# Compact states, paired outputs in rows of token parity with the bonus on TensorE, and a new order, in a chunked linear-attention kernel followed by a two-layer MLP

## The chip, the cores and the metric

The kernel runs on one core of a Trainium2 chip. The metric is the device time of one execution in microseconds (us). Engines are named as in the profile: PE (TensorE, matrix products; PEld are its weight loads), DVE (VectorE), ACT (ScalarE), POOL (GpSimd), SP (SyncE, which issues most DMAs). [...]

## The reference

B = 4 batches, H = 8 heads, S = 768 tokens, D = 48 columns a head; then an MLP of 384 -> 2048 -> 384 over 3072 tokens.

```python
state = zeros(B, H, D, D)
for t in range(S):
    cur = einsum('bhd,bhe->bhde', u[None] * k[t], v[t])
    y[t] = einsum('bhd,bhde->bhe', r[t], state + cur)
    state = w * state + einsum('bhd,bhe->bhde', k[t], v[t])
x = y, tokens as rows, heads side by side        # 3072 x 384
h = x @ w_in
g = where(h >= 1, h, where(h <= -1, 0, (h + 1)**2 / 4))
out = g @ w_out
```

## The kernel before

Tokens are cut into chunks of 128. A **group** is 256 tokens, and there are twelve. Groups 0 to 3 are **paired**: group g holds the first two chunks of batch g, with two neighbouring tokens (2q and 2q+1) in the same row; an index e or f of 2 is the parity of the token, and `un` (rows 0 to 63 or 64 to 127) tells the first chunk from the second. Groups 4 to 11 are unpaired: one chunk (c = 2 to 5) of each of two batches, index j.

The kernel's work is written as small steps, `step_X(e, s, g, ...)`. Their order is a list written out in the string `ORDER` (lines 32 to 67): a token such as `RU2@D` or `T0.0#3` is a step, its group (and half or quarter), after @ the engine (D VectorE, A ScalarE, P GpSimd) and after # one of four PSUM slots of two banks. Every engine runs its own instructions strictly in the order of this list, and each waits for what it reads and for the buffer that it writes. The steps of a group:

- `ldK`, `ldV`, `ldR`: loads, issued by SP in list order. `Vc`: V to bf16 (`Vb`).
- `Rs`, `Ks`: R and K times powers of the decay w, to bf16 (`RK`). `KU` = K times u, `RU` = R times KU, `us` sums RU over a head, `ud` = V times that sum: the bonus (`V2`). Group 0 is done in halves (.0 and .1).
- `T`, `TT`: RK transposed on TensorE, and copied out of PSUM (`RKT`). From group 4 on, `RK` does it with a DMA transpose.
- `A`, `AT`: products of K and R within a chunk, then masked on VectorE to bf16.
- `Sp`: K-transposed times V, the chunk's addition to the state, four pairs of heads. A pair is computed as one 96 x 96 block, so half of it, where the heads differ, is not wanted; `wCm` (the decay over a chunk) is zero there, and the product with it clears it. `Ta` (paired: first chunk's state), `Tm` (Sp plus state), `dc` (Tm times wCm) keep the state; `sa`, `sb` copy it to bf16.
- `Y`: the output of the group in PSUM: state part plus AT times Vb. `y` adds the bonus on VectorE, to bf16. `X`, `xT`: y transposed by TensorE (groups 0 to 3) or by DMA.
- `up` g.q: a quarter of the first layer, 12 matmuls of 256 columns; `re`, `sq` on ScalarE and `ga` on VectorE make the activation; `dn` g.j.q: four matmuls of 384 columns of the second layer; `o` copies out of PSUM, `st` stores.
- `wi`, `wo`: halves of w_in and w_out, loaded and converted by DMAs of GpSimd's queue. `kw`n: n matmuls of zeros, which write nothing that is used. `wr`, `ur`, `wB`, `uB`, `uc`, `ln`, `wu`, `wd`, `lp`, `lc`, `wc`: the tables of the decay and of u, from rows loaded on ScalarE's queue and spread by TensorE; `wB`, then `ln`, give log w, `wu` and `wd` the powers, `lc` and `wc` the chunk's decay `wCm`.

In a paired group, Y stands in PSUM with rows (chunk, q) and columns by parity f, so that a row of `out` for tokens 2q and 2q+1 lies in one partition.

Of the kernel before, what the change touches and what calls it, by code (L numbers as in the profile page):

```python
# [26 lines left out]

ORDER = """  # L30
wr@A ldK0.0 ldV0 ldR0.0 ur@A tb kw16#0 wB#0 uB#1 ln wu0 uc@D KU0.0@P wd1 wd0 wu1 lp ldK0.1 KU0.1@D Rs0.0@D RU0.0@P
Ks0.0@D kw20#2 lc#2 wc us0.0 ldR0.1 RU0.1@D ldR1 us0.1 Rs1@D Vc0@A ldK1 kw6#0 T0.0#3 Ks0.1@P Rs0.1@P kw13#0 T0.1#1
TT0.0@A TT0.1@A A0.0#0 Ks1@D Sp0#2 Ta0 ldV1 vu AT0.0 Vc1@A A0.1#3 Tm0 AT0.1 ud0.0@P ud0.1@D T1.0#1 TT1.0@A A1.0#0
sa0@A Y0.0#2 y0.0 Y0.1#1 y0.1 T1.1#3 TT1.1@D wi0 Sp1#2 Ta1 Tm1 AT1.0 wi1 wo0 KU1@P X0#1 dc0@P A1.1#3 AT1.1 sb0@A xT0@A
sa1@P up0.0#1 up0.1#2 Y1#0 RU1@P us1 ud1@D y1 up0.2#3 up0.3#0 re0.0 sq0.0 re0.1 sq0.1 ga0.0 ga0.1 X1#1 xT1@D up1.0#2
up1.1#1 re0.2 sq0.2 ga0.2 dc1@P sb1@P ldK2 KU2@P re0.3 sq0.3 dn0.0.0#3 dn0.1.0 dn0.1.1 ldR2 re1.0 sq1.0 Rs2@P Ks2@D
ga0.3 ga1.0 RU2@D re1.1 sq1.1 ga1.1 T2.0#0 TT2.0@A ldV2 Vc2@P up1.2#2 re1.2 Sp2#0 wo1 up1.3#1 ldR3 Rs3@P ldR4 Ta2 Tm2
dn0.0.1 ldR5 dn1.0.0#0 dn1.0.1 sq1.2 ga1.2 re1.3 sq1.3 us2 sa2@P ga1.3 T2.1#2 ldK3 dn1.1.0 dn1.1.1 A2.0#1 AT2.0
TT2.1@A A2.1#2 AT2.1 ldK4 dn0.0.2 dn0.0.3 dn1.1.2 dn1.0.2 Y2#1 Ks3@D ud2@P Rs4@P dc2@D y2 Rs5@P vd T3.0#2 TT3.0@D
dn1.1.3 dn1.0.3 o0.0@A o1.0@A KU3@P RU3@D X2#1 xT2@A A3.0#2 AT3.0 ldV3 Vc3@A o1.1@A dn0.1.2 dn0.1.3 Ks4@P us3 T3.1#1  # L40
TT3.1@A Sp3#2 o0.1@D Ta3 Tm3 up2.0#0 KU4@P A3.1#3 AT3.1 ldV4 Vc4@P Sp4#1 ud3@P RU4@P Tm4 up2.1#2 re2.0 sa3@A sq2.0
ga2.0 Y3#3 y3 re2.1 sq2.1 up2.2#1 up2.3#0 re2.2 X3#3 sq2.2 ga2.1 xT3@D us4 ldK5 dn2.0.0#2 dn2.0.1 up3.0#3 dn2.1.0
Ks5@P ga2.2 RK4 st0 ldV5 RK5 A4.0#1 re2.3 sq2.3 ldR6 dn2.1.1 ga2.3 A4.1#0 dc4@P sb2@P dc3@P dn2.1.2 dn2.0.2 re3.0
sq3.0 dn2.0.3 AT4.0 AT4.1 dn2.1.3 KU5@P RU5@P Y4#1 us5 up3.1#0 Vc5@A ga3.0 A5.0#3 st1 ud4@P y4 o2.0@A o2.1@A sb3@P
A5.1#2 re3.1 sq3.1 AT5.0 AT5.1 ldK6 up3.2#1 xT4 up3.3#3 ga3.1 dn3.0.0#2 dn3.1.0 sb4@P Rs6@P Y5#0 re3.2 sq3.2 ga3.2
dn3.0.1 dn3.0.2 ud5@D y5 up4.0#1 re3.3 sq3.3 ga3.3 ldK7 ldR7 dn3.1.1 Sp5#0 KU6@P Ks6@P KU7@P RU6@P up4.1#3 re4.0 sq4.0
re4.1 sq4.1 dn3.1.2 dn3.0.3 dn3.1.3 Tm5 ga4.0 us6 ga4.1 o3.0@A up4.2#0 o3.1@A RK6 A6.0#1 AT6.0 A6.1#2 re4.2 sq4.2
up4.3#3 AT6.1 xT5 up5.0#1 up5.1#2 RU7@P dc5@P ldV6 re4.3 sq4.3 ga4.2 ga4.3 us7 Rs7@P Vc6@P re5.0 sq5.0 ud6@P Ks7@D
dn4.0.0#0 dn4.1.0 dn4.1.1 dn4.1.2 dn4.0.1 ldR8 dn4.1.3 up5.2#3 dn4.0.2 dn4.0.3 st3 re5.1 sq5.1 Rs8@D ga5.0 ga5.1 Y6#1
y6 ldV7 st2 ldK8 re5.2 sq5.2 ga5.2 Ks8@D RK7 Vc7@P o4.0@A o4.1@A up5.3#2 re5.3 sq5.3 Sp6#0 dn5.0.0#1 dn5.0.1 dn5.1.0  # L50
dn5.1.1 A7.0#3 dn5.0.2 Tm6 sb5@A ud7@P KU8@P RU8@P dc6@P A7.1#0 ga5.3 xT6 up6.0#2 AT7.0 AT7.1 Sp7#3 dn5.0.3 ldV8 sb6@A
Y7#0 Tm7 re6.0 sq6.0 y7 dn5.1.2 dn5.1.3 Vc8@P o5.0@A Sp8#3 o5.1@A ga6.0 RK8 up6.1#0 re6.1 sq6.1 ldK9 Tm8 A8.0#1 AT8.0
A8.1#2 AT8.1 xT7 up6.2#3 re6.2 up6.3#1 dn6.0.0#2 dn6.1.0 sq6.2 ga6.1 us8 re6.3 sq6.3 ga6.2 ga6.3 ldR9 Rs9@D dn6.1.1
up7.0#0 re7.0 sq7.0 Y8#3 dn6.0.1 up7.1#1 KU9@P ud8@P st4 ldK10 re7.1 sq7.1 ga7.0 y8 ga7.1 RU9@P ldR10 Rs10@D dn6.0.2
dn6.0.3 up7.2#0 re7.2 dn6.1.2 o6.0@D Ks9@P RK9 up7.3#3 sq7.2 re7.3 sq7.3 ga7.2 dc8@P dc7@P sb7@P dn7.0.0#1 dn7.0.1
dn7.1.0 KU10@P dn6.1.3 o6.1@A A9.0#0 dn7.0.2 A9.1#2 dn7.1.1 ga7.3 dn7.0.3 xT8 up8.0#3 dn7.1.2 dn7.1.3 Ks10@P AT9.0
AT9.1 us9 ldV9 Vc9@P st5 o7.0@D o7.1@D ud9@P sb8@P Y9#0 y9 re8.0 sq8.0 ga8.0 up8.1#2 Sp9#1 Tm9 up8.2#0 up8.3#3 re8.1
dn8.0.0#1 dn8.1.0 ldR11 Rs11@P dc9@D st6 sq8.1 ga8.1 ldK11 RU10@D re8.2 sq8.2 xT9 ga8.2 us10 ldV10 re8.3 RK10 sq8.3
up9.0#2 dn8.0.1 up9.1#0 dn8.1.1 dn8.1.2 ga8.3 dn8.0.2 st7 Ks11@P KU11@P RU11@P RK11 A10.0#3 dn8.0.3 us11 re9.0 sq9.0
ga9.0 A10.1#2 AT10.0 AT10.1 dn8.1.3 re9.1 sq9.1 o8.0@A up9.2#3 re9.2 o8.1@D ga9.1 Vc10@P ud10@P Y10#2 y10 up9.3#1  # L60
sq9.2 re9.3 sq9.3 dn9.0.0#0 dn9.1.0 dn9.0.1 A11.0#2 dn9.1.1 ga9.2 sb9@A ldV11 Vc11@A A11.1#3 dn9.1.2 AT11.0 AT11.1
xT10 up10.0#2 re10.0 sq10.0 dn9.0.2 ga9.3 Y11#3 ud11@P y11 xT11 ga10.0 up10.1#1 dn9.0.3 up10.2#3 re10.1 dn9.1.3 o9.0@D
o9.1@D sq10.1 st8 st9 re10.2 ga10.1 sq10.2 ga10.2 up10.3#2 re10.3 sq10.3 ga10.3 up11.0#0 re11.0 sq11.0 dn10.0.0#1
dn10.1.0 dn10.1.1 dn10.0.1 dn10.0.2 up11.1#3 up11.2#2 re11.1 sq11.1 ga11.0 ga11.1 dn10.0.3 dn10.1.2 up11.3#0 re11.2
sq11.2 re11.3 sq11.3 ga11.2 dn10.1.3 dn11.0.0#3 dn11.1.0 dn11.0.1 o10.0@D o10.1@A st10 dn11.0.2 dn11.1.1 dn11.1.2
ga11.3 dn11.0.3 dn11.1.3 o11.0@A st11.0 o11.1@A st11.1
# [4 lines left out]
def kernel(  # L71
# [174 lines left out]
    def step_wu(e, s, i):  # L246
        if i == 0:
            nc.scalar.activation(flat(W2[0][:, 0]), lw, AF.Exp, scale=up2_col)
        else:
            nc.vector.tensor_mul(flat(W2[0][:, 1]), flat(W2[0][:, 0]), got("wB"))  # L250

    def step_wd(e, s, i):
        if i == 1:
            nc.scalar.activation(flat(W2[1][:, 1]), lw, AF.Exp, scale=dn2_col)
# [12 lines left out]
    def step_lc(e, s):  # L267
        col = bank(s, "lcol", (), [P, NP], F32)
        for p in range(NP):
            nc.tensor.matmul(col[:, p : p + 1], lwp[:, p].rearrange("q i d -> q (i d)"), ones[:, :1], start=True, stop=True)  # L270
# [8 lines left out]

    def step_wi(e, s, i):  # L280
        n = slice(i * DF // 2, (i + 1) * DF // 2)
        nc.gpsimd.dma_start(out=w_in_sb[:, :, n], in_=w_in_src[:, :, n])

    def step_wo(e, s, i):
        n = slice(i * nF // 2, (i + 1) * nF // 2)
        nc.gpsimd.dma_start(out=w_out_sb[:, n, :], in_=w_out_src[:, n, :])
# [83 lines left out]
    def step_A(e, s, g, h):  # L370
        t = got("RKT", g)
        if g in PAIRED:
            A = bank(s, "A", (g, h), [P, 2, NP // 2, 2, P], F32)
            for p in range(NP // 2):
                for e2 in range(2):
                    for i in range(2):
                        ps = slice(i * HP, i * HP + D)
                        for un in range(2):
                            q = slice(un * HP, (un + 1) * HP)
                            nc.tensor.matmul(  # L380
                                A[q, i, p, e2].rearrange("p (e q) -> p e q", e=2), t[ps, 1, e2, 2 * h + p, q], t[ps, 0, :, 2 * h + p, q], start=True, stop=True,
                                skip_group_check=True,
                            )
# [212 lines left out]
```

## Time and profile before

| | |
|---|---|
| median of 3 runs | 184.1 us (183.78 to 186.46) |
| profiled execution | 184.28 us; its span 182.5 us |
| hp (`up`), PE | 576 matmuls, 69.0 us busy |
| op (`dn`), PE | 384 matmuls, 69.4 us busy |
| gt (`ga`), VectorE | 48 instructions, 57.8 us busy |
| pt and sq (`re`, `sq`), ScalarE | 96 instructions, 99.6 us busy |
| granted TensorE clock | 0.999 |

The page gives each engine's busy time over the span. The windows give the same by stretch. The chain that ended last follows the program back from its last instruction: at each step to what released it, or to the instruction before it on its engine; merged pieces are given as start, length, what and how many. Busy times of matmuls overlap: each is counted with its whole passage through the array, so the cost of one in a row is read from the chain, where a piece of n matmuls takes its share of the time alone.

### The profile page before, as it was taken

Reading aid. Unit: us, or ns where it says so; the run is one execution under the profiler, and the core shown is the slowest. Engines: PE = TensorE matmul, PEld = TensorE weight load, DVE = VectorE, ACT = ScalarE, POOL = GpSimd, SP = SyncE. Lnnn points to the kernel's source line nnn. Section 1 sums busy time; section 2 is a strip of 40 time slices with the busy share of each in tenths; the row PEclk is TensorE's granted clock in tenths of the full one; section 3 lists DMA queues with packets and bytes.
Section 4 is the critical chain, followed back from the end, with each engine's and each line's share of the span. In section 5 each row is a group of like instructions: output and inputs, shape, how many; then the busy total and the mean of one; then the engine's idle time right before and its main releaser. Section 6 shows DMA issues by size and latency. Waiting matters only on the chain.

```text
span 182.5 us, 4612 instructions
## 1 busy us (share of the span) xinstructions
PE 170.5 (93%) x1963; PEld 128.2 (70%) x1963; DVE 152.4 (84%) x163; ACT 123.4 (68%) x139; POOL 111.2 (61%) x85
## 2 busy tenths in 40 slices
...
GB/s 156 313 311 163 191 202 140 128 150 229 192 40 223 115 205 89 165 169 182 258 172 71 160 185 230 146 71 219 270 85 240 176 71 47 0 190 30 0 88 86
...
## 3 DMA queue, kind: packets, MB, share of 16 engines
...
q0 software_dynamic: 2880, 3.15, 11.1%
...
## 4 chain that ended last, share of the span: by engine, by line
PE 65%; DVE 14%; issue 9%; DMA 5%; POOL 4%; ACT 1%; ACTq 0%; POOLq 0%; DVEq 0%
PE op L538 28%; PE hp L516 27%; DVE gt L531 6%; DMA w_in_sb<-in_moe_w_in_dram 5%; PE A L389 3%; DVE RK L312 2%; DVE y L494 2%; PE Y L484 1%; PE Y L481 1%; PE Y L474 1%; DVE RU L327 1%; POOL RK L312 1%; PE Sp L418 1%; DVE AT L395 1%; POOL V L340 1%
## 5 line engine op out<-in xcount | busy, mean ns | idle before, releaser
L516 PE MATMUL hp<-xT,w_in_sb 128*128 128x256 bf16 x576 | 69.0, 273 | 4.1 <-DVE gt L531 1.8
L538 PE MATMUL op<-w_out_sb,gt 128*128 128x384 bf16 x384 | 69.4, 326 | 0.0
L523 ACT ACTIVATE pt<-hp 128x1024 f32<-128x1024 f32 x48 | 48.8, 1017 | 24.7 <-PE hp L516 24.6
L516 PEld LDWEIGHTS <-w_in_sb 128*128 128x128 bf16 x576 | 55.1, 98 | 13.3 <-issue 3.2
L531 DVE SCALAR_TENSOR_TENSOR gt<-sq,hp 128x1024 bf16<-128x1024 f32 x48 | 57.8, 1213 | 7.5 <-ACT sq L527 7.5
L527 ACT ACTIVATE sq<-pt 128x1024 f32<-128x1024 f32 x48 | 50.8, 1058 | 1.7 <-DVE gt L531 0.2
L538 PEld LDWEIGHTS <-gt 128*128 128x128 bf16 x384 | 36.2, 98 | 21.0
L321 POOL TENSOR_TENSOR KU<-K,u_bc 128x768 f32<-128x768 f32 (+1 forms) x12 | 23.9, 1990 | 8.4 <-DMA K<-in_k_dram 5.1
L340 POOL TENSOR_TENSOR V<-Vb,us 128x768 f32<-128x768 bf16 (+1 forms) x10 | 15.4, 1540 | 17.3 <-ACT Vb L120 9.8
L401 DVE TENSOR_TENSOR AT<-A,mask 128x1024 bf16<-128x1024 f32 x16 | 18.8, 1216 | 2.1 <-PE A L389 2.1
L327 POOL TENSOR_TENSOR RU<-R,KU 128x768 f32<-128x768 f32 (+1 forms) x9 | 17.5, 1951 | 0.3
L120 ACT COPY o<-op 128x384 f32<-128x384 f32 x16 | 7.1, 477 | 14.6 <-PE op L538 14.6
L494 DVE TENSOR_TENSOR y<-Y,V 128x768 bf16<-128x768 f32 (+1 forms) x13 | 11.5, 891 | 3.5 <-issue 1.1
L312 POOL TENSOR_TENSOR RK<-R,W 128x768 bf16<-128x768 f32 (+1 forms) x8 | 14.0, 1756 | 0.2 <-DMA R<-in_r_dram 0.2
L447 POOL TENSOR_TENSOR state<-Tm,wCm 128x768 f32<-128x768 f32 (+1 forms) x8 | 12.0, 1508 | 2.9 <-DVE Tm L441 2.9
L312 POOL TENSOR_TENSOR RK<-K,W 128x768 bf16<-128x768 f32 (+1 forms) x7 | 12.9, 1848 | 0.4 <-DMA K<-in_k_dram 0.4
L120 POOL CAST state_bf<-state 128x384 bf16<-128x384 f32 (+1 forms) x8 | 5.6, 698 | 11.7 <-DVE state L428 8.2
L333 DVE TENSOR_REDUCE us<-RU 128x16 f32<-128x768 f32 (+1 forms) x13 | 11.5, 882 | 0.9 <-POOL RU L327 0.9
L395 DVE TENSOR_TENSOR AT<-A,mask 128x1024 bf16<-128x1024 f32 x8 | 9.6, 1216 | 0.7 <-PE A L380 0.7
L312 DVE TENSOR_TENSOR RK<-K,W 128x768 bf16<-128x768 f32 (+1 forms) x6 | 8.6, 1432 | 0.0
L312 DVE TENSOR_TENSOR RK<-R,W 128x768 bf16<-128x768 f32 (+1 forms) x5 | 8.0, 1594 | 0.0
L294 PE MATMUL idle<-warm 128*128 128x128 bf16 x55 | 6.6, 313 | 1.0 <-DVE warm L136 1.0
...
## 6 DMA issues: line engine op xcount, KB each, us to landing
...
w_out_sb<-in_moe_w_out_dram POOLq DMA_DIRECT2D x2, 768.0 KB, 11.5
...
```

Source lines behind the costliest of these rows:

```text
L120: nc.scalar.copy(out, in_) if e == "A" else engines[e].tensor_copy(out, in_)
L312: engines[e].tensor_mul(RK[g % NB][:, x, :, hs, :D], rows(got(what, g), g)[:, :, hs], table(x, g, hs))
L321: engines[e].tensor_mul(got("KU", g)[:, :, hs], rows(got("K", g), g)[:, :, hs], u_rep)
L327: engines[e].tensor_mul(got("RU", g)[:, :, hs], rows(got("R", g), g)[:, :, hs], got("KU", g)[:, :, hs])
L340: engines[e].tensor_mul(got("V2", g)[:, :, hs], got("Vb", g)[:, :, hs], sums)
L401: nc.vector.tensor_mul(t.rearrange("p i n t -> p (i n) t"), got("A", g, h).rearrange("p i n t -> p (i n) t"), mask)
L494: nc.vector.tensor_add(got("y", g)[:, :, cols], got("Y", g, part)[:, :, : cols.stop - cols.start], got("V2", g).rearrange("p j h d -> p j ...
L516: nc.tensor.matmul(hp[:, f].rearrange("p (j t) -> p j t", j=2), w_in_sb[:, i, n0 : n0 + P], got("xT", g)[:, :, i, :], start=(i == 0), stop ...
L523: nc.scalar.activation(t, got("hp", g, q), AF.Relu, bias=0.5, scale=0.5)
L527: nc.scalar.activation(t, got("pt", g, q), AF.Square)
L531: nc.vector.scalar_tensor_tensor(out=t, in0=got("sq", g, q), scalar=1.0, in1=got("hp", g, q), op0=ALU.min, op1=ALU.max)
L538: nc.tensor.matmul(got("op", g)[:, j, :DO], got("gt", g, q)[:, f, j * P : (j + 1) * P], w_out_sb[:, n, :], start=(n == 0), stop=(n == nF - 1),
```

## The change

- States hold 48 columns a pair of heads instead of 96: the first head of the pair in partitions 0 to 47, the second in 64 to 111. `Sp` is computed a head at a time (64 columns of the array, 48 moving columns), `Ta`, `Tm`, `dc`, `sb` and `wCm` are half as wide. Unpaired `Y` takes the state part a head at a time (48 rows of the array), all of it ahead of the AT products, and its PSUM tile has the heads of a pair in different banks.
- Paired `Y` stands in PSUM with rows (parity f, q) and columns by chunk `un`. The AT products of both parities go in one matmul (64 x 128), the state part as a full matmul on `sd`, a block-diagonal bf16 copy of the state that `sa` writes in two copies, and the bonus is added by TensorE: `V2`, now bf16, through a part of the identity. `y` is then a copy out of PSUM, on the engine that the order names. `RKT` of a paired group has its parities side by side, `TT` copies in that order, and `st` is two DMAs, one a chunk.
- Tables: the second `wu` or `wd` may be an exp on ScalarE; `lc` runs two idle matmuls behind each of its own.
- `ORDER` is new throughout. The halves of `w_in` and `w_out` are as before (`W_IN_ENDS`, `W_OUT_ENDS`).

The first lines of both orders, up to the first `up`:

```diff
-wr@A ldK0.0 ldV0 ldR0.0 ur@A tb kw16#0 wB#0 uB#1 ln wu0 uc@D KU0.0@P wd1 wd0 wu1 lp ldK0.1 KU0.1@D Rs0.0@D RU0.0@P
-Ks0.0@D kw20#2 lc#2 wc us0.0 ldR0.1 RU0.1@D ldR1 us0.1 Rs1@D Vc0@A ldK1 kw6#0 T0.0#3 Ks0.1@P Rs0.1@P kw13#0 T0.1#1
-TT0.0@A TT0.1@A A0.0#0 Ks1@D Sp0#2 Ta0 ldV1 vu AT0.0 Vc1@A A0.1#3 Tm0 AT0.1 ud0.0@P ud0.1@D T1.0#1 TT1.0@A A1.0#0
-sa0@A Y0.0#2 y0.0 Y0.1#1 y0.1 T1.1#3 TT1.1@D wi0 Sp1#2 Ta1 Tm1 AT1.0 wi1 wo0 KU1@P X0#1 dc0@P A1.1#3 AT1.1 sb0@A xT0@A
-sa1@P up0.0#1 up0.1#2 Y1#0 RU1@P us1 ud1@D y1 up0.2#3 up0.3#0 re0.0 sq0.0 re0.1 sq0.1 ga0.0 ga0.1 X1#1 xT1@D up1.0#2
+ldK0.0 wr@A ldR0.0 ldV0 ldK0.1 tb ur@A kw16#0 wB#0 ln lp wu0@A wd1@A wd0@A wu1@D Rs0.0@D Ks0.1@P Vc0@A Ks0.0@D kw25#1
+uB#1 uc@A KU0.0@D T0.0#2 Sp0#3 ldR0.1 Rs0.1@D ldK1 ldR1 KU0.1@D lc#0 wc RU0.0@D T0.1#1 wi0 us0.0 TT0.0@A Ta0 RU0.1@P
+sa0@A Rs1@D us0.1 A0.0#0 TT0.1@A kw16#2 A0.1#2 ud0.0@P ldV1 AT0.0 AT0.1 Y0.0#1 y0.0@A ud0.1@P kw9#0 Y0.1#0 Ks1@D Vc1@A
+Sp1#2 KU1@D Tm0 T1.0#1 TT1.0@D y0.1@A X0#0 xT0@D Ta1 T1.1#3 A1.0#1 Tm1 ldK2 wi1 up0.0#0 TT1.1@A RU1@P us1 AT1.0 A1.1#2
+AT1.1 wo0 up0.1#3 re0.0 sq0.0 ga0.0 re0.1 ud1@P sq0.1 sa1@P dc1@P sb1@P Y1#1 y1@D vu up0.2#2 re0.2 sq0.2 X1#0 up0.3#1
+xT1@D KU2@P ga0.1 ga0.2 re0.3 sq0.3 up1.0#0 re1.0 sq1.0 ga0.3 ga1.0 wo1 up1.1#3 up1.2#2 dn0.0.0#1 re1.1 sq1.1 re1.2
+sq1.2 ldR2 ldR3 RU2@P Rs2@P Ks2@P ldR4 dn0.0.1 dn0.1.0 dn0.1.1 ldV2 T2.0#0 dn0.1.2 us2 dn0.1.3 dn0.0.2 dn0.0.3 Rs3@D
...
```

The engines that the two lists give to the whole products (halves of group 0 left out): `Ks` on VectorE for groups 1, 2, 3, 7, 8 before and 1, 3 after; `Rs` 1, 8, 9, 10 before and 1, 3 after; `RU` 2, 3, 10 before and none after; `KU` none before and 1 after; `ud` 1, 5 before and 6, 9 after; `dc` 2, 9 before and 8 after. The others are on GpSimd. `y` is on ScalarE for groups 0 and 3 after, on VectorE otherwise.

The core of the steps:

```diff
-    states = [const.tile([P, 2, NP, 2 * D], F32, name="state", tag=f"st{b}") for b in range(BP)]
+    states = [const.tile([P, 2, NP, D], F32, name="state", tag=f"st{b}") for b in range(BP)]
+    sd = [const.tile([P, NP, 2 * D], BF16, name="sd", tag=f"sd{i}") for i in range(ROOM["sd"])]
+    for t in sd:
+        nc.gpsimd.memset(t, 0.0)
...
     def step_Sp(e, s, g):
-                        nc.tensor.matmul(
-                            Sp[:, un, cols], RK[g % NB][q, 1, e2, hs, :].rearrange("p h d -> p (h d)"),
-                            flat(got("Vb", g)[q, e2, hs, :]), start=(e2 == 0), stop=(e2 == 1), skip_group_check=True,
-                        )
+                    for i in range(2):
+                        for un in range(2):
+                            q = slice(un * HP, (un + 1) * HP)
+                            nc.tensor.matmul(
+                                Sp[i * HP : (i + 1) * HP, un, cols], K[q, 1, e2, 2 * p + i, :], V[q, e2, 2 * p + i, :],
+                                start=(e2 == 0), stop=(e2 == 1), skip_group_check=True,
+                            )
...
+    def step_sa(e, s, g):
+        for i in range(2):
+            ps = slice(i * HP, i * HP + D)
+            copy(e, sd[g % len(sd)][ps, :, i * D : (i + 1) * D], state_of(g, states)[ps])
...
     def step_Y(e, s, g, part=None):
+        if g in PAIRED:
+            S, V2 = sd[g % len(sd)], got("V2", g)
+            for p in range(h0 // 2, hs.stop // 2):
+                nc.tensor.matmul(Y[:, 1, cols], t[:, p // 2, 0, p % 2, 1].rearrange("d f q -> d (f q)"), S[:, p, :], start=(2 * p == h0), stop=False, skip_group_check=True)
+            for h in range(h0, hs.stop):
+                for e2 in range(2):
+                    for un in range(2):
+                        nc.tensor.matmul(
+                            Y[:, un, (h - h0) * D : (h + 1 - h0) * D], got("AT", g, p // 2)[q, i, p % 2, e2, :], V[q, e2, h, :],
+                            start=(un == 0 and e2 == 0 and h == h0), stop=False, skip_group_check=True,
+                        )
+            for f in range(2):
+                for un in range(2):
+                    nc.tensor.matmul(
+                        Y[f * HP : (f + 1) * HP, un, :n], ident[q, q], V2[q, f, hs, :].rearrange("q h d -> q (h d)"), start=False, stop=True,
+                        skip_group_check=True,
+                    )
+            return
...
+        if goes_on:
+            for j in range(2):
+                for p in range(NP):
+                    for i in range(2):
+                        ps = slice(i * HP, i * HP + D)
+                        nc.tensor.matmul(
+                            Y[:, i, j, p, :], t[ps, 0, j, p, :], S[ps, j, p, :], start=(j == 0 and p == 0), stop=False,
+                            skip_group_check=True,
+                        )
```

More of the change, by code (lines that the diff above doesn't have):

```diff
@@ L26 @@
 T_BY_DMA, X_BY_DMA = 4, 4
+W_IN_ENDS, W_OUT_ENDS = [2, 4], [2, 4]
 ORDER = """
[L31 to L39, printed above, removed]
@@ L65 @@
-sq11.2 re11.3 sq11.3 ga11.2 dn10.1.3 dn11.0.0#3 dn11.1.0 dn11.0.1 o10.0@D o10.1@A st10 dn11.0.2 dn11.1.1 dn11.1.2
-ga11.3 dn11.0.3 dn11.1.3 o11.0@A st11.0 o11.1@A st11.1
+ldK0.0 wr@A ldR0.0 ldV0 ldK0.1 tb ur@A kw16#0 wB#0 ln lp wu0@A wd1@A wd0@A wu1@D Rs0.0@D Ks0.1@P Vc0@A Ks0.0@D kw25#1
+uB#1 uc@A KU0.0@D T0.0#2 Sp0#3 ldR0.1 Rs0.1@D ldK1 ldR1 KU0.1@D lc#0 wc RU0.0@D T0.1#1 wi0 us0.0 TT0.0@A Ta0 RU0.1@P
+sa0@A Rs1@D us0.1 A0.0#0 TT0.1@A kw16#2 A0.1#2 ud0.0@P ldV1 AT0.0 AT0.1 Y0.0#1 y0.0@A ud0.1@P kw9#0 Y0.1#0 Ks1@D Vc1@A
@@ new lines @@
+Sp1#2 KU1@D Tm0 T1.0#1 TT1.0@D y0.1@A X0#0 xT0@D Ta1 T1.1#3 A1.0#1 Tm1 ldK2 wi1 up0.0#0 TT1.1@A RU1@P us1 AT1.0 A1.1#2
+AT1.1 wo0 up0.1#3 re0.0 sq0.0 ga0.0 re0.1 ud1@P sq0.1 sa1@P dc1@P sb1@P Y1#1 y1@D vu up0.2#2 re0.2 sq0.2 X1#0 up0.3#1
+xT1@D KU2@P ga0.1 ga0.2 re0.3 sq0.3 up1.0#0 re1.0 sq1.0 ga0.3 ga1.0 wo1 up1.1#3 up1.2#2 dn0.0.0#1 re1.1 sq1.1 re1.2
+sq1.2 ldR2 ldR3 RU2@P Rs2@P Ks2@P ldR4 dn0.0.1 dn0.1.0 dn0.1.1 ldV2 T2.0#0 dn0.1.2 us2 dn0.1.3 dn0.0.2 dn0.0.3 Rs3@D
+Rs4@P Vc2@P dc0@P ga1.1 ga1.2 TT2.0@A T2.1#3 TT2.1@D A2.0#0 up1.3#2 o0.0@A o0.1@A ud2@P ldR5 ldK3 ldK4 A2.1#1 AT2.0
@@ L337, in step_ud @@
         if first:
-            new("V2", (g,), [P, 2, H, D], F32)
+            new("V2b" if g in PAIRED else "V2", (g,), [P, 2, H, D], BF16 if g in PAIRED else F32)
+            live[("V2", g)] = got("V2b" if g in PAIRED else "V2", g)
         sums = got("us", g)[:, :, hs].unsqueeze(3).to_broadcast([P, 2, hs.stop - hs.start, D])
```

216 lines of the change are left out of this document (103 added, 113 removed).

## Prediction

> **What bounds the kernel now.** I read the page first, then the windows, then the chain that ended last, in order of time.
>
> ```profile
> span 182.5 us, 4612 instructions
> PE 170.5 (93%) x1963; PEld 128.2 (70%) x1963; DVE 152.4 (84%) x163; ACT 123.4 (68%) x139; POOL 111.2 (61%) x85
> ```
>
> TensorE is nearly always busy, but that is a mean over stages: VectorE at 84% is close behind, and a window shows where it takes over (stretch and length, then busy us of PE, PEld, DVE, ACT, POOL).
>
> ```profile
> 30.00:35.00 5.00, 4.28 (x39) 3.42 (x38) 5.00 (x5) 4.94 (x6) 3.90 (x4) 1.00 0.59 74
> ```
>
> Here TensorE is idle for 0.72 us while VectorE has no gap at all. The chain gives the price of each TensorE step when nothing holds it up (start, us, what):
>
> ```profile
> 22.98 2.79 PE hp L516 x24
> ...
> 54.22 0.45 PE T L352 x8
> 54.67 0.45 PE Sp L412 x16
> ...
> 56.53 0.35 PE A L380 x16
> 56.88 0.45 PE Sp L418 x8
> 57.32 1.31 PE hp L516 x12
> 58.63 0.46 PE Y L463 x8
> 59.09 1.12 PE Y L474 x64
> ...
> 62.94 0.34 PE X L502 x6
> 63.27 1.30 PE op L538 x8
> ...
> 67.95 2.71 PE op L538 x16
> ...
> 71.40 1.31 PE hp L516 x12
> 72.71 0.55 PE A L389 x16
> ...
> 178.48 0.48 ACT o L120
> ```
>
> So the span has three parts. Prelude: 22.98 us until the first `hp`. Tail: from the last matmul at 178.48 to 182.5, 4.0 us. Between them 155.5 us, of which TensorE needs: 48 `up` of 1.31 and 96 `dn` of 0.65, 125.3; `Y1` and `X1`, 1.6 + 0.3; groups 2 and 3, each two T, two A, Sp, Y, X = 0.90 + 0.70 + 0.45 + 1.58 + 0.34 = 4.0, so 7.9; groups 4 to 9, each A, Sp and Y, where an unpaired Y takes 0.74 (the op ends at 70.66, the next hp starts at 71.40) = 1.74, so 10.4; groups 10 and 11, 1.3 each, 2.6. Sum 148.1. Hence 7.4 us are lost between the first hp and the last matmul. Only four things can move the time: the prelude, the work of TensorE, these 7.4 us, the tail.
>
> **VectorE and GpSimd: where the 7.4 us come from.** The timeline of both engines:
>
> ```profile
> 46.90 1.89 DVE L312 TENSOR_TENSOR RK<-K,W 128x768 bf16<-128x768 f32 x1
> 48.71 2.17 DVE L447 TENSOR_TENSOR state<-Tm,wCm 128x384 f32<-128x384 f32 x1
> ...
> 58.98 1.22 DVE L531 SCALAR_TENSOR_TENSOR gt<-sq,hp 128x1024 bf16<-128x1024 f32 x1
> ...
> 122.38 2.43 DVE L312 TENSOR_TENSOR RK<-R,W 128x768 bf16<-128x768 f32 x1
> ```
> ```profile
> 47.92 2.54 POOL L321 TENSOR_TENSOR KU<-K,u_bc 128x768 f32<-128x768 f32 x1
> ...
> 58.98 1.83 POOL L312 TENSOR_TENSOR RK<-K,W 128x768 bf16<-128x768 f32 x1
> ```
>
> A product of two SBUF tiles on VectorE delays GpSimd and is delayed by it: the 384-column `dc2` takes 2.17 us beside a KU that takes 2.54. A `ga`, which reads one of its operands in PSUM, does neither: the RK beside it takes 1.83. [...]
>
> Counted in the two orders (halves of group 0 as halves), VectorE's products go from 16.5 (Rs 4.5, Ks 5.5, KU 0.5, RU 3.5, ud 2.5) to 10 (3, 2.5, 2, 0.5, 2), and its two dc to one; GpSimd gets them. Behind group 3 VectorE keeps three (`ud6`, `dc8`, `ud9`) of eight. At the 1.89 and 2.43 us of the rows above, 6.5 products and a dc are 14 to 18 us of VectorE. Compact states halve their instructions:
>
> ```profile
> L447 POOL TENSOR_TENSOR state<-Tm,wCm 128x768 f32<-128x768 f32 x5 | 9.0, 1814 | 2.9 <-DVE Tm L441 2.9
> ...
> L441 DVE TENSOR_TENSOR Tm<-Sp,state 128x768 f32<-128x768 f32 x6 | 5.7, 952 | 0.6 <-PE Sp L418 0.5
> ...
> L447 POOL TENSOR_TENSOR state<-Tm,wCm 128x384 f32<-128x384 f32 x3 | 3.0, 998 | 0.0
> ...
> L438 DVE TENSOR_TENSOR Tm<-Sp,state 128x384 f32<-128x384 f32 x4 | 2.2, 555 | 0.1
> ```
>
> Six Tm go from 952 to 555 ns, 2.4 us of VectorE; five dc on GpSimd from 1814 to 998, 4.1 us of GpSimd, which pay for two of the products that it gets. The paired y becomes a copy out of PSUM of as many columns, on ScalarE (68% busy) for groups 0 and 3: 0 on VectorE for the others, bounds -0.3 and +0.3 each. All this lies beside TensorE; it is worth only what it gives back of the 7.4 us. The losses behind 45 us follow on `dc2`, the late RK and their like, which leave VectorE: I take back 4 us. The rest lies near 30 to 40 us, where a new wait arises (below): 3.4 us stay, bounds 1.5 and 6.
>
> Four small edits, with the rows that price them:
>
> ```profile
> 1.42 0.31 POOL L168 MEMSET mask<- 128x256 f32 x1
> ...
> 39.65 0.50 POOL L120 CAST state_bf<-state 128x384 bf16<-128x384 f32 x1 [5.73 <-DVE state L428]
> ...
> 55.85 0.37 SPq L554 DMA_DIRECT2D out_dram<-o  x1
> ```
>
> Two clears of `sd` (128x384, bf16) join GpSimd's set-up, at 0.2 to 0.5 us each; it is idle then until about 6.5 us: 0. The paired `sa` becomes two copies of 48x192 instead of one of 128x384 at 0.50: together 0.4 to 1.0. Before, a Y waited for it just so; 0, and 0.5 a group where GpSimd is late. The two extra column operations of VectorE replace the clear of the wider `wCm`: 0. A paired store becomes two DMAs: SP's queue holds 0.4 us more, four times, with loads queued behind; these were issued groups ahead: 0, and 1.6 if a load were due. The copy out of T writes runs of 64 columns in a new place, as many columns as before: 0.
>
> **TensorE's own work.** Nothing of up, dn, T, A, X changes. An L474 matmul (64x64, 48 columns) costs 1.12/64 = 18 ns; an L418 one (128x128, 96 columns) 0.45/8 = 56 ns; an L412 one (64x128, 96 columns) 28 ns; the 128x128 ones of an unpaired Y, 24 of them in 0.74 us, 31 ns.
> - Paired Sp: 32 of 64x64 instead of 16 of 64x128: 32 x 18 = 0.57 against 0.45; bounds 0.45 and 0.9 (28 ns). Three behind the first hp: +0.4.
> - Unpaired Sp: 16 of 128x64 at 48 columns; between 18 and 31 ns, 0.29 to 0.5 against 0.45: 0.
> - Paired Y: 4 full ones at up to 56 ns, 0.2; 32 of 64x128 between 18 and 28 ns, 0.6 to 0.9; the bonus, four 384-column matmuls on four quarters of the array: at a `dn`'s rate (1.30/8) 0.16 if they run together, 0.65 one by one. Sum 1.0 to 1.75 against 1.58; I take 1.3, nearer the L474 row, which shows quarters overlapping. Three of them: -0.8.
> - Unpaired Y: 32 instead of 24; the added eight at 18 to 34 ns (0.55/16 for A's 48-row matmuls), with possibly a gap where the shape changes: 0.8 to 1.05 against 0.74; I take 0.86. Eight: +1.0.
> Sum +0.6 (bounds -2 and +5): 148.7.
>
> [...]
>
> **Prelude.**
>
> ```profile
> 4.38 1.48 PE L238 MATMUL uB<-u_row,ones 1*128 1x384 f32 x2
> ...
> 5.66 0.60 ACT L254 ACTIVATE W<-lw,dn_col 128x384 f32<-128x384 f32 x1
> 5.79 2.31 PE L294 MATMUL idle<-warm 128*128 128x128 bf16 x20
> ...
> 8.16 1.86 PE L270 MATMUL lcol<-ones,lwp 1*128 1x1 f32 x8
> ...
> 11.67 1.01 ACT L120 COPY RKT<-T 128x1024 bf16<-128x1024 bf16 x1
> ...
> 13.69 1.71 POOL L282 DMA_DIRECT2D w_in_sb<-in_moe_w_in_dram  x2
> ...
> 15.65 1.22 DVE L395 TENSOR_TENSOR AT<-A,mask 128x1024 bf16<-128x1024 f32 x1
> ...
> 21.04 0.80 ACT L120 COPY xT<-X 128x768 bf16<-128x768 bf16 x1 [1.39 <-PE X L502]
> ```
>
> Before, xT0 was ready at 21.84 and the first hp still waited for w_in until 22.98. In the new order `wi0` stands behind one GpSimd half product only, which needs the table that is now a third exp on ScalarE (6.26 + 0.6 = 6.9): it is issued near 8 us instead of 13.69, and that wait goes. But xT0 hardly comes earlier. uB moves behind 25 warm matmuls (2.31/20 x 25 = 2.9 us): 4.4 + 2.9 + 1.5 = 8.9. KU0.0 on VectorE waits for it, with Rs0.1, KU0.1, RU0.0, Ta0 queued behind. `lc` (1.86, and eight warm matmuls, 0.9) now stands ahead of T0.1, and `wc` ahead of TT0.0 on ScalarE: T0.0 and Sp0 to about 10.8, lc 13.6, wc 14, TT0.0 1.01 to 15, so AT0.0 starts near 15.5, as before (15.65). The second half follows as before: sa0 and TT0.1 to 16.7, AT0.1 to 18.4, Y0.1 to 19.1, y0.1 behind Vc1 on ScalarE to 19.7, and xT0 on VectorE behind Ks1, KU1, Tm0, TT1.0 near 21.5 to 22. First hp: 21.9, bounds 20.5 and 23.5.
>
> **Weights.** Four DMAs of 768 KB leave GpSimd's queue:
>
> ```profile
> 31.13 0.94 POOL L286 DMA_DIRECT2D w_out_sb<-in_moe_w_out_dram  x1
> ...
> DMA to landing us min/median/max: 7.0/11.5/15.9
> ```
>
> The 7.0 is this one's (landed 38.1, the DMAs being free). In the new order `wo1` follows KU2, near 28 us. The first product that needs it, `dn0.1.2`, comes after 7 up, 4 dn, Y1, X1, A1.1 and T2.0 = 9.2 + 2.6 + 1.3 + 0.3 + 0.35 + 0.45 = 14.2 us, at 36 us. Issued at 28 it lands at 35 to 40: a stall of 0 to 4, 1.5 of which I have in the 3.4.
>
> **GpSimd's own path.** A new wait: a paired Y adds the bonus on TensorE, so Y, and all that is queued behind it, waits for `ud`, as only VectorE's y did. From KU1's end (20.5 us by the walk above) GpSimd runs RU1, ud1, KU2, RU2, Rs2, Ks2 (1.83 each, the ud less) and two weight issues (0.94), about 13 us with the small state steps: T2.0 may start at 33.5; TensorE gets there at 35.7. Margins of 2 to 5 us stay in later groups: no stall, if a product takes 1.83.
>
> **Tail.** At the end one o copy of 0.48 instead of two stands behind the last matmul: 3.6.
>
> Sum: 21.9 + 148.7 + 3.4 + 3.6 = 177.6 us. The profiled execution took 184.28 for its span of 182.5, so 1.8 more: 179.4. The median of the three runs, 184.1, is as near to that execution as makes no difference: 2.6% faster.
>
> **Rivals.** (1) The weights come late: `wo1` takes the 15.9 us of the slowest, lands at 44, and dn0.1.2 waits 7.8 instead of 1.5: 185.7; with the median of 11.5, 181.3. For it: nine input loads share the DMAs; against: they were free at 31 us. Near 183. (2) Small matmuls cost their upper bounds: +4.4, 183.8; against it speaks the 18 ns row. (3) Slower: GpSimd becomes the bound. From KU2 to Ks7 it has 20 products and four ud; if they take the 2.54 of the KU above because VectorE's copies and one-SBUF ops hold it as well, that is 24 x 0.7 = 17 us, less the 5 of margin: 12 us of stall, 191.4. It decides from 0.2 us a product on. The 1.83 beside `ga` speaks against it. (4) The change does less than it says, because nothing was VectorE's: the 7.4 us stay, 183.4. (5) More is won: first hp at 20.5, 1.5 lost: 176.1.
>
> **Numbers.** Forecast 0.58, its own range 177 to 182.5; (1) 0.12, (2) 0.06, (3) 0.10, (4) 0.07, (5) 0.07. Under 2% either way a measurement can't be told from no change: the marks are 180.4 and 187.8. Two thirds of the forecast and (5) lie below: faster 0.47; slower (3) and the edge of (1): 0.12; same 0.41. Range 176 to 187: it leaves out (3) and little else.
>
> **What would show it.** First hp near 22 and not waiting for a DMA; no VectorE product above 1.3 us behind 55 us; POOL products at 1.83; TensorE idle between first hp and last matmul under 2.5 us. It is wrong if PE waits for w_out_sb beyond 38 us, if POOL ends the waits of T, A or Y, or if Sp and Y groups exceed 0.9 and 1.75 us.

## The result, and the profile after

The changed kernel takes 200.7 us (median of 4 runs, 198.39 to 202.38) where the kernel before takes 183.9: a ratio of 1.089 [1.075, 1.102], so 8.9% slower. The forecast was 179.4, and its range ended at 187. The profiled execution took 201.26 us for a span of 199.5. (Some executions of every kernel here are 1 to 3 us slower than its others; the profiled one of the first experiment, at 187.05, is such a one.)

The page, with the busy time of each engine:

```profile
span 199.5 us, 4766 instructions
...
PE 174.6 (88%) x2034; PEld 125.4 (63%) x2034; DVE 130.1 (65%) x153; ACT 122.9 (62%) x143; POOL 111.1 (56%) x97
```

VectorE has lost 22 us of work (152.4 before), as the change intended, and the span has grown by 17 us all the same. No engine became the bound: the share of each has fallen. That alone says to look for a wait on something that is not an engine. The chain that ended last names it by engine (before, DMA had 5% of it):

```profile
PE 57%; DMA 22%; ACT 6%; DVE 5%; POOL 3%; issue 3%; SPq 2%; POOLq 0%; ACTq 0%; DVEq 0%
```

and the view of waits gives the instructions that stood (engine, line and what it waited for; us in total, times, longest):

```profile
POOL RK L325 <- DMA K<-in_k_dram: 11.5, 3, 6.1
POOL RK L325 <- DMA R<-in_r_dram: 9.7, 3, 4.8
...
PE hp L550 <- DMA xT<-y: 8.0, 2, 7.8
POOL Vb L123 <- DMA V<-in_v_dram: 7.7, 3, 5.2
...
PE A L401 <- DMA RKT<-RK: 3.2, 2, 2.1
```

Loads of K, R and V and both kinds of DMA transpose come late, though what each of them moves is unchanged; the new order only issues them at other times. Before, the longest wait for a load of K, R or V in the whole trace was this one, of 3.5 us, and none for a transpose stands in that view:

```profile
POOL KU L321 <- DMA K<-in_k_dram: 5.1, 2, 3.5
```

What stands ahead of the late ones is seen in SP's queue (start, us, line, operation):

```profile
76.02 0.57 SPq L229 DMA_DIRECT2D K<-in_k_dram  x1
76.69 1.78 SPq L589 DMA_DIRECT2D out_dram<-o  x2
78.52 2.45 SPq L229 DMA_DIRECT2D R<-in_r_dram  x1
81.09 8.69 SPq L381 DMA_TRANSPOSE RKT<-RK  x1
89.83 1.15 SPq L589 DMA_DIRECT2D out_dram<-o  x2
91.08 5.09 SPq L543 DMA_TRANSPOSE xT<-y  x1
```

Each pair of L589 is the store of a paired group in its new form. Behind it the issue of a transpose holds SP for 8.69 us. The windows show what the DMA engines do in that time (the last two columns are their mean busy share, of 16, and GB/s):

```profile
84.00:86.00 2.00, 2.00 (x18) 1.61 (x17) 0.87 (x1) 0.69 (x2) 0.53 (x1) 1.00 0.13 50
86.00:88.00 2.00, 1.73 (x15) 1.30 (x14) 0.24 (x1) 0.83 (x1) 0.00 (x0) 1.00 0.14 43
...
96.00:98.00 2.00, 0.00 (x0) 0.00 (x0) 0.43 (x1) 0.00 (x0) 2.00 (x1) 0.51 0.13 50
98.00:100.00 2.00, 0.00 (x0) 0.00 (x0) 0.95 (x1) 0.00 (x0) 0.09 (x1) 0.50 0.13 51
```

The share is 0.13 and the rate 50 GB/s, in stretches in which loads and transposes are waiting. 2/16 is 0.125, what two busy engines and fourteen idle ones would show. The packet records of the trace fit it: from 84 to 86 us exactly two packets are under way for 88% of the time, each 1536 bytes, a row of the output. Which engines carry them, the trace doesn't tell. The two stores of a group are 2 x 192 KB, which at 50 GB/s is 7.9 us. The chain has the price of that (start, us from the start of the issue, what):

```profile
81.09 9.99 DMA RKT<-RK
91.08 10.30 DMA xT<-y
...
101.42 5.14 PE hp L550 x24
```

Twenty microseconds of the chain are two transposes; the median RKT took 4.4 us before, with 6.2 the longest. The third row is a second bill: after 7.8 us without work TensorE's granted clock stands at 0.50, and 24 hp take 5.14 us that took 2.79 in the chain of before.

Why two: the store writes rows (parity, q) to tokens 2q + parity, so its access to DRAM, `[[DO, 2], [2 * DO, HP], [1, DO]]`, has the parity as the slowest dimension, of size 2. That the two packets under way come from this 2 is my estimate, from the share of 0.13 and the size; the first experiment changes this dimension and keeps the bytes.

### The profile page after: what moved, and what is told of

Its sections match the earlier page's. It is cut to its first block, busy times and chain, and to the rows that moved or that the text cites. A ratio compares the mean times of both kernels' runs of the same rounds, so it can differ in the third digit from the quotient of the medians.

```text
span 199.5 us, 4766 instructions
## 1 busy us (share of the span) xinstructions
PE 174.6 (88%) x2034; PEld 125.4 (63%) x2034; DVE 130.1 (65%) x153; ACT 122.9 (62%) x143; POOL 111.1 (56%) x97
## 4 chain that ended last, share of the span: by engine, by line
PE 57%; DMA 22%; ACT 6%; DVE 5%; POOL 3%; issue 3%; SPq 2%; POOLq 0%; ACTq 0%; DVEq 0%
PE op L572 23%; PE hp L550 18%; DMA xT<-y 7%; DMA w_out_sb<-in_moe_w_out_dram 5%; DMA R<-in_r_dram 5%; DMA RKT<-RK 5%; PE idle L307 4%; ACT pt L557 3%; ACT sq L561 2%; DVE gt L565 2%; PE A L401 1%; PE Y L515 1%; PE A L395 1%; PE T L366 1%; POOL RK L325 1%
## 5 line engine op out<-in xcount | busy, mean ns | idle before, releaser
L325 POOL TENSOR_TENSOR RK<-K,W 128x768 bf16<-128x768 f32 (+1 forms) x10 | 18.4, 1843 | 15.2 <-DMA K<-in_k_dram 11.5
L340 POOL TENSOR_TENSOR RU<-R,KU 128x768 f32<-128x768 f32 (+1 forms) x12 | 21.9, 1822 | 5.1 <-DVE KU L334 4.6
L325 POOL TENSOR_TENSOR RK<-R,W 128x768 bf16<-128x768 f32 x9 | 16.4, 1819 | 9.7 <-DMA R<-in_r_dram 9.7
L334 POOL TENSOR_TENSOR KU<-K,u_bc 128x768 f32<-128x768 f32 x10 | 18.2, 1819 | 0.1
L530 DVE TENSOR_TENSOR y<-Y,V 128x768 bf16<-128x768 f32 x8 | 7.6, 956 | 13.7 <-PE Y L515 11.9
L354 POOL TENSOR_TENSOR V<-Vb,us 128x768 f32<-128x768 bf16 x6 | 8.9, 1479 | 13.3 <-DVE us L346 13.2
L346 DVE TENSOR_REDUCE us<-RU 128x16 f32<-128x768 f32 (+1 forms) x13 | 11.5, 884 | 1.7 <-POOL RU L340 1.7
L123 POOL CAST Vb<-V 128x768 bf16<-128x768 f32 x7 | 5.8, 827 | 7.8 <-DMA V<-in_v_dram 7.7
L401 PE MATMUL A<-RKT 48*128 48x128 bf16 x128 | 6.0, 218 | 3.2 <-DMA RKT<-RK 3.2
L123 ACT COPY RKT<-T 128x1024 bf16<-128x1024 bf16 x6 | 6.0, 1009 | 4.6 <-PE T L366 4.5
L401 PEld LDWEIGHTS <-RKT 48*128 48x128 bf16 x128 | 3.6, 94 | 7.3 <-DMA RKT<-RK 3.9
```

Source lines behind the costliest of these rows:

```text
L123: nc.scalar.copy(out, in_) if e == "A" else engines[e].tensor_copy(out, in_)
L325: engines[e].tensor_mul(RK[g % NB][:, x, :, hs, :D], rows(got(what, g), g)[:, :, hs], table(x, g, hs))
L334: engines[e].tensor_mul(got("KU", g)[:, :, hs], rows(got("K", g), g)[:, :, hs], u_rep)
L340: engines[e].tensor_mul(got("RU", g)[:, :, hs], rows(got("R", g), g)[:, :, hs], got("KU", g)[:, :, hs])
L401: nc.tensor.matmul(A[:, i, p, :], t[ps, 1, h, p], t[ps, 0, h, p], start=True, stop=True)
```

## Experiments: the store

**The changed kernel with a store that isn't narrow.** The same bytes in two DMAs as well, but cut by parity, so that the slowest dimension is q (64):

```diff
-            for un in range(2):
-                dst = bass.AP(tensor=out.tensor, offset=out.offset + (r0 + un * C) * DO, ap=[[DO, 2], [2 * DO, HP], [1, DO]])
-                nc.sync.dma_start(out=dst, in_=o[:, un])
+            for f in range(2):
+                dst = bass.AP(tensor=out.tensor, offset=out.offset + (r0 + f) * DO, ap=[[2 * DO, HP], [C * DO, 2], [1, DO]])
+                nc.sync.dma_start(out=dst, in_=o[f * HP : (f + 1) * HP])
```

> The changed kernel with the paired store cut the other way: still two DMAs of 192 KB a group with the same rows of 1536 bytes, but one a parity (64 partitions, both chunks) instead of one a chunk (parity as the outermost dimension, of 2). Theory A, the stores: an access whose outermost dimension is 2 runs on 2 of the 16 DMA engines, 0.13 of them at some 50 GB/s, for about 8 us a group, and the loads and transposes behind it wait for those two engines. Then the stretches of 0.13 go, R<-in_r lands in under 7 us where it took 10.7, and the time falls from 200 to 177 to 183 us, near the forecast. Theory B, the order: it issues loads and transposes too late on SP's queue, whatever the stores are. Then the time stays above 195 us and GpSimd still waits more than 20 us for DMAs. Between 184 and 195: both.

Measured: 185.0 us (183.41 to 188.21, 10 runs), 1.004 [0.999, 1.009] of the kernel before. Of the 16.8 us lost, the shape of the store was 15.7; but 185.0 is above theory A's 177 to 183, so the store isn't all that the forecast missed. That there are two DMAs a group instead of one doesn't matter: here are two as well. A window that holds the stores of one group, issued at 83.33:

```profile
82.00:84.00 2.00, 2.00 (x31) 1.64 (x31) 1.06 (x2) 1.17 (x2) 2.00 (x2) 1.00 1.21 253
```

TensorE's wait for xT falls from 8.0 us to 0.3, and GpSimd's for R from 9.7 to 1.5. Its wait for K hardly falls, so most of that row of the changed kernel isn't the store's doing:

```profile
POOL RK L325 <- DMA K<-in_k_dram: 9.1, 2, 6.2
```

**The kernel before with the narrow store alone.** Nothing else of the change is in it; the rows of groups 0 to 3 land at other tokens, and the bytes are as many:

```diff
-            dst = out[g * S : g * S + 2 * C, :].rearrange("(p e) d -> p e d", e=2)
-            nc.sync.dma_start(out=dst, in_=o)
+            for un in range(2):
+                dst = bass.AP(tensor=out.tensor, offset=out.offset + (g * S + un * C) * DO, ap=[[DO, 2], [2 * DO, HP], [1, DO]])
+                nc.sync.dma_start(out=dst, in_=o[:, un])
```

> The kernel before with the changed kernel's paired store alone: two DMAs a group whose outermost dimension is 2. The rows of groups 0 to 3 land at other tokens of the output; every byte is still written once. Theory A: stretches of DMA share 0.13 appear behind the four stores (56 to 90 us) and the time rises by 4 to 15 us, depending on what waits behind them. Theory B: no change, 183 to 186 us.

Measured: 201.3 us (199.89 to 202.4), 1.093 [1.083, 1.102]: 17 us more, above the 4 to 15 expected. So the store costs as much in an order and with steps that have nothing to do with the change. The windows and the chain show the same two signs:

```profile
80.00:82.00 2.00, 2.00 (x33) 1.27 (x29) 1.90 (x3) 1.55 (x2) 0.00 (x0) 1.00 0.13 51
```
```profile
73.26 10.66 DMA K<-in_k_dram
...
107.68 10.64 DMA RKT<-RK
```

The K at 73.26 is issued just behind a store pair of 71.29.

**Two narrow stores, in place and late.** Both runs are the changed kernel with the wide store for groups 0 and 1, the narrow one for groups 2 and 3, and two output buffers of their own for these:

```diff
+        if g in (2, 3):
+            for un in range(2):
+                dst = bass.AP(tensor=out.tensor, offset=out.offset + (r0 + un * C) * DO, ap=[[DO, 2], [2 * DO, HP], [1, DO]])
+                nc.sync.dma_start(out=dst, in_=o[:, un])
```

In the second they are issued behind the last transpose of y:

```diff
-y11@D xT11 dn9.1.3
+y11@D xT11 st2 st3 dn9.1.3
```

> The changed kernel with the wide store for groups 0 and 1 and the narrow one for groups 2 and 3, at their usual places in the order, with two output buffers of their own. Theory A (each narrow store costs what its later loads and transposes wait, about 4 us a group): 191 to 195 us, half of the loss. Rival B (the loss comes of one store, or of the first two, where loads are shortest of time): within 2 us of 185 or of 200.

> As the run with two narrow stores, but these stand behind the last transpose of y (near 158 us), so that no load or transpose is queued behind them; only output is. Two groups at about 8 us each end near 175 us. Theory A (a narrow store costs only through the loads and transposes behind it): 184 to 187 us, as with wide stores, with at most 2 us from the last stores. Rival B (the narrow transfers cost by themselves, through memory or through TensorE's operands): 191 to 195 us as at the usual places.

Measured: in place 195.0 us (191.41 to 196.01, 4 runs), late 185.8 (185.51 to 188.13; 1.016 [1.006, 1.026] of the kernel before). The transfers are the same; only what is queued behind them differs. In place two groups cost between 6 and 11 us beside the wide stores' 185.0, as theory A has it; the four runs are too far apart to tell half of the loss from two thirds. Late they run for some 8 us a group as well (384 KB at 45 to 52 GB/s between 162 and 170 us), and from 160 to 168 us TensorE is busy all the while:

```profile
162.00:164.00 2.00, 2.00 (x18) 1.55 (x16) 1.22 (x1) 1.97 (x3) 0.00 (x0) 1.00 0.13 45
```

The 0.9 us that the late run has over the wide stores' 185.0 is within the spread of both. Its trace has a wait that may hold them, where a later output store stands behind the narrow ones and the last copy but one waits for its buffer:

```profile
ACT o L123 <- DMA out_dram<-o: 2.8, 1, 2.8
```

**Another queue.** The changed kernel, its narrow stores issued by ScalarE instead of SP:

```diff
-                nc.sync.dma_start(out=dst, in_=o[:, un])
+                nc.scalar.dma_start(out=dst, in_=o[:, un])
```

> The changed kernel as it is, with its narrow stores (two DMAs a paired group), but issued on ScalarE's queue in place of SP's; nothing else is moved. Theory A (the loads and transposes of SP's queue wait because they use the same two DMA engines, whichever queue the store came from): 198 to 203 us, as the changed kernel's 200.7, with ScalarE holding its next instruction at most 1 us a store. Rival B (they wait because SP's queue is served in order, so that a store on another queue shares the engines and its bytes no longer stand ahead of a load's): 188 to 195 us.

Measured: 202.5 us (200.56 to 203.9), 1.100 [1.089, 1.110]: no better. The chain still has a load and a transpose, and now a store too:

```profile
76.73 11.28 DMA out_dram<-o
89.76 7.08 DMA V<-in_v_dram
96.84 14.87 DMA RKT<-RK
```

The store is there because a copy `o` waits for the buffer that it empties:

```profile
DVE o L123 <- DMA out_dram<-o: 4.7, 1, 4.7
```

So the wait isn't the order of SP's queue. That leaves the DMA engines: that the stores of both queues meet the loads and transposes on the same ones is my estimate, from 202.5 us here against 200.7. How a load is spread over the engines, and which of them carry a store, no run here shows.

## Experiments: the rest of the change

With a wide store the change still brings nothing: 185.0 against the 179.4 forecast. The next runs ask where the gain went.

**The new steps under the old order**, with the wide store; `Y1` and `Y2` are moved behind their `ud`, which they now read, and y stays on VectorE:

```diff
-sa1@P up0.0#1 up0.1#2 Y1#0 RU1@P us1 ud1@D y1 up0.2#3
+sa1@P up0.0#1 up0.1#2 RU1@P us1 ud1@D Y1#0 y1@D up0.2#3
```

> All new steps (compact states, parity rows, bonus on TensorE) with the wide store of the first run, under the order of the kernel before; Y1 and Y2 are moved behind their ud, y on VectorE. It parts the steps from the order. By the terms of the forecast: TensorE within 1 us of before, Tm and dc shorter by 6 us off its path, the prelude as before: 181 to 185 us. If the steps themselves hold a cost that the forecast missed: above 187.

Measured: 185.0 us (184.05 to 187.7), 1.006 [1.001, 1.011], the upper end of what the terms of the forecast gave. Neither the steps alone nor the steps with the new order gain anything.

In the trace of the wide store (first experiment) the first hp starts at 23.37 and the last matmul ends at 181.65: 158.3 us. By the prices that TensorE's steps show now (next section) its work there is about 146.1, so 12.2 us are lost, more than the 7.4 before. The timeline of TensorE shows three places (start, us, instruction, in brackets how long it stood idle and for what):

```profile
72.62 0.82 PE L572 MATMUL op<-w_out_sb,gt 128*128 128x384 bf16 x4 [1.41 <-DVE gt L565]
...
170.60 3.78 PE L572 MATMUL op<-w_out_sb,gt 128*128 128x384 bf16 x12 [2.13 <-DVE o L123]
...
180.80 0.81 PE L572 MATMUL op<-w_out_sb,gt 128*128 128x384 bf16 x4 [0.57 <-ACT o L123]
```

In each a copy `o` out of PSUM is ahead of a product in the order. The second costs most: `o10.0` on VectorE stands behind `ga11.0` and `ga11.1`, and `dn10.1.1` behind it in the list waits for it. Here it costs again afterwards, for 12 op take 3.78 us; in the five us behind 170 the granted clock was 0.66. That isn't the rule: in the profile of the changed kernel the same 12 op stand behind an idle time of 2.12 us, and the clock stays at 1.00:

```profile
186.46 2.11 PE op L572 x12
```

All three can be moved:

```diff
-Tm5 o2.0@D o2.1@A
+Tm5 o2.0@A o2.1@A
...
-re11.2 o10.0@D sq11.2
+re11.2 sq11.2
...
-dn11.0.1 o10.1@D st10
+dn11.0.1 o10.0@D o10.1@D st10
...
-dn11.0.3 o11.0@A st11.0 dn11.1.3 o11.1@A
+dn11.0.3 dn11.1.3 o11.0@A st11.0 o11.1@A
```

> The changed kernel with the store cut by parity (185.0 us), and three steps of its order moved: o2.0 goes from VectorE to ScalarE; o10.0 goes behind dn10.1.1 to dn10.1.3 (to just ahead of o10.1); dn11.1.3 goes ahead of o11.0. Theory A: what the rest of the change won (7.4 us lost between the first hp and the last matmul before) was given back at three places of the new order, where a copy out of PSUM stands in the way: 1.4 us idle at 72.6, 2.1 us idle and about 1.8 us of lower clock behind 170.6, 0.6 us at the end. Then 179 to 182 us. Rival B: the places are only where a shortage shows, and ScalarE's chain (98 to 107 and 159 to 171 us) or the late warm-up of TensorE's clock sets the end: 184 to 186 us.

> As the run with three moves, with the two moves at the end alone (o10.0 behind dn10.1.3, dn11.1.3 ahead of o11.0); o2.0 stays on VectorE. Theory A: 1 to 2 us above the run with all three, 180.5 to 183 us. Rival B: no difference from 185 us.

Measured: with all three 181.8 us (179.56 to 182.68, 6 runs), 0.985 [0.977, 0.993]; with the two at the end alone 181.6 (180.69 to 183.93, 4 runs), 0.987 [0.979, 0.995]. Both lie where theory A put them. The end of the order had cost some 3 us. The move of o2.0 cuts its wait from 1.4 to 0.3 us in the trace, but 1 us is less than the spread of these runs, and the medians don't show it. These two are the fastest versions of the study, 1.3 to 1.5% below the kernel before: clear of no change, but less than 2%. With three moves TensorE's part of the chain has no break from 150 us to the last copy:

```profile
165.06 1.95 PE op L572 x12
167.01 1.31 PE hp L550 x12
168.32 5.21 PE op L572 x32
173.56 0.48 ACT o L123
```

**The prelude.** The profiled execution of the run with three moves took 179.56 us, the fastest of its six and 2.3 less than their median. The timeline of TensorE shows where such a difference can come from. First this run, then the wide store with the same first lines of the order:

```profile
4.51 2.85 PE L307 MATMUL idle<-warm 128*128 128x128 bf16 x25
7.41 1.14 PE L248 MATMUL uB<-u_row,ones 1*128 1x384 f32 x2
8.49 0.62 PE L366 MATMUL T<-ident,RK 128*128 128x128 bf16 x8
```
```profile
4.51 2.85 PE L307 MATMUL idle<-warm 128*128 128x128 bf16 x25
7.42 1.64 PE L248 MATMUL uB<-u_row,ones 1*128 1x384 f32 x2
8.99 1.03 PE L366 MATMUL T<-ident,RK 128*128 128x128 bf16 x8
```

The same matmuls, and within uB TensorE's rate rises in the one and not in the other. `lc` follows at the two rates, T0.1 starts at 11.47 or at 13.74, and the first hp at 21.1 or at 23.4: the lead of 2.3 us is won by 11.5 us and kept. The high rate doesn't last. From 12 to 18 us the windows of the first trace have the granted clock at 0.50 (the number behind POOL's), and T0.1 takes 1.06 us in both:

```profile
14.00:16.00 2.00, 1.94 (x30) 1.72 (x28) 1.13 (x1) 0.58 (x1) 1.57 (x2) 0.50 1.12 209
```

What decides when the rate rises, these two traces don't show. Two runs tried to make the early rise certain, both from the kernel with three moves: eight more idle matmuls ahead of uB, and uB ahead of the idle matmuls.

```diff
-Ks0.0@D kw25#1 uB#1 uc@A
+Ks0.0@D kw33#1 uB#1 uc@A
```
```diff
-wB#0 ln lp
+wB#0 uB#1 kw25#2 ln lp
```

> The run with three moves (median 181.8 us, fastest 179.6) with 33 idle matmuls in place of 25 ahead of uB. In the traces so far TensorE runs the steps behind uB either at full speed (T0.0 0.55 us, first hp near 21.1) or at half (T0.0 0.97 us, first hp near 23.3), from one execution to the next. Theory A: the clock rises only after a stretch of full matmuls, which uB (one row of weights, 1.64 us) interrupts too early in some executions; eight more, 0.9 us, make it rise in nearly all: 180 to 181 us, with less spread. Rival B: the rise doesn't hang on these matmuls, and the eight come on top: 182 to 183 us.

> The run with three moves, with uB ahead of the 25 idle matmuls, so that these run from 5.9 to 8.7 us and T0.0 follows them without a break. Theory A (a stretch without uB in it makes the clock rise early and so the prelude short in nearly all executions): 179.5 to 181 us. Rival B (the idle matmuls start too late for the rise, or it doesn't hang on them): 181.5 to 183.5 us, T0.0 at 0.97 us.

Measured: 182.2 us (181.27 to 183.44) and 182.8 (181.29 to 183.97), 0.989 [0.983, 0.995] and 0.990 [0.985, 0.995]. Neither helped. In the profiled execution with 33 idle matmuls the rise is late all the same (T0.0 1.03 us, first hp at 23.9). With uB first the rise is early, within T0.0 (0.99 us; Sp0 behind it 0.44, where 33 idle matmuls have 0.63), and T0.1 takes 0.61 us; but then the clock stands at 5 tenths in the two slices from 13.5 to 22.5 us, and the first hp starts at 23.3 (below, the page's row of the granted clock in tenths, in 40 slices of 4.5 us):

```profile
12.08 0.61 PE L366 MATMUL T<-ident,RK 128*128 128x128 bf16 x8
```
```profile
PEclk9995599999999999999999999999999999999999
```

So an early rise alone didn't make the prelude short: with the clock back at 0.50 from 12 to 18 us (three moves) the first hp starts at 21.1, with 5 tenths in these two slices at 23.3. Theory A isn't confirmed; what sets the rise and the fall stays open.

## Why the prediction was wrong

**The step that failed** is the fourth of the small edits: "A paired store becomes two DMAs: SP's queue holds 0.4 us more, four times, with loads queued behind; these were issued groups ahead: 0, and 1.6 if a load were due." It measured 15.7 us, the difference between the narrow store and the wide one. I counted the instructions and their time in the issuing queue, and took the transfer itself for unchanged because its bytes are. I read the new access pattern only for where the rows go, not for the rate that it gives, here 50 GB/s. That what is behind a store is "issued groups ahead" was wrong too: the transposes RKT and xT stand in the same queue, and TensorE waited 7.8 us for one of them. No rival held this mechanism.

**The sum, by its own terms.** The execution with the wide store and three moves can be set beside it:

| | forecast | there |
|---|---|---|
| first hp | 21.9 | 21.1 |
| TensorE's work behind it | 148.7 | 146.1 |
| lost | 3.4 | 6.4 |
| tail | 3.6 | 4.2 |
| around the span | 1.8 | 1.8 |
| sum | 179.4 | 179.6 |

That the sums agree is partly luck: this is the fastest of six executions, two terms miss in opposite directions, and the order isn't the one that was forecast. TensorE's work is worked out from the chain, which shows a paired Sp, a paired Y in its three parts and, from group 4 on, an unpaired Y and Sp in the changed kernel:

```profile
45.11 0.25 PE Sp L426 x32
...
47.41 0.17 PE Y L481 x4
47.58 0.51 PE Y L487 x32
48.09 0.29 PE Y L494 x4
...
66.18 0.36 PE Sp L433 x16
...
106.56 0.30 PE Y L508 x16
106.87 0.52 PE Y L515 x16
```

A paired Y takes 0.97 us and not 1.3 (three: -1.0), a paired Sp 0.25 to 0.37 and not 0.57 (-0.8), an unpaired Sp 0.36 and not 0.45 (six: -0.5), an unpaired Y 0.82 and not 0.86 (eight: -0.3): 148.7 - 2.6, about 146.1. Four matmuls of 384 columns on the four quarters of the array take 0.29 us, between the 0.16 and the 0.65 that I had.

The lost time is the term that was mis-sized the other way: 6.4 in this execution, and 12.2 in the profile of the order as it is, 1.7 of it the slower 12 op. I took back 4 us because VectorE's products leave; they did leave, and in the order as it is new waits took their place, among them the copies `o`. For those I had looked only at the last one and booked a gain of 0.4. The 7.4 us was also no measure of waiting. The windows count TensorE busy for 151.5 of the 155.5 us before, so it was idle for 4.0; the rest is matmuls that took longer than the prices of the sum. It was idle for 5.3 us with the wide store and for 1.4 with three moves: only there is it under the 2.5 us that the prediction named as a sign.

**What was right.** The first hp of the changed kernel starts at 20.8 us and waits for no DMA. GpSimd's products don't slow down, and VectorE's are no longer held up. By form, in the changed kernel:

```profile
L325 DVE TENSOR_TENSOR RK<-K,W 128x768 bf16<-128x768 f32 x2 | 1.9, 973 | 0.0
```
```profile
L334 POOL TENSOR_TENSOR KU<-K,u_bc 128x768 f32<-128x768 f32 x10 | 18.2, 1819 | 0.1
```

The product took VectorE 1.89 us in the row of before and takes 0.97 now, and the products that it keeps behind 55 us take 1.06 (`ud6` and `ud9`, their mean) and 0.55 (`dc8`); GpSimd's products with K and R stay between 1.82 and 1.94 on average. So rival 3 falls, and rival 2 with the prices above. Rival 1 is there in small: in the changed kernel TensorE waits 2.4 us for w_out at 38 us, not in the execution of the table. Rival 4, nothing gained, is what the wide store alone shows, but not for its reason: VectorE did give up 22 us of work, and the end of the order cost some 3 us again.
